# Products of identities in TensorE's planned gaps, and a planner with a changed clock model

## The chip, the cores and the metric

The kernel is one program on one core of a Trainium2 chip. The metric is its device time in microseconds. Four of the core's engines matter here: TensorE (PE, matrix products), VectorE (DVE), ScalarE (ACT) and SyncE (SP, which only issues DMAs). Each runs its own instructions strictly in the order in which the program lists them, and waits on semaphores for the others.

## The reference, cut to what matters

An attention with a local window and a few global rows feeds an MLP with the Mish activation:

```
B, H, Sl, D = 8, 8, 512, 64;  Sg = 32;  window 32
out_g = softmax(q_g k_all^T / 8) v_all                     # 32 global queries see all 544 keys
out_l = softmax([q_l k_g^T | banded q_l k_l^T] / 8) [v_g | v_l]
x     = concat(out_g, out_l) as rows of (B * 544, 512)
h     = x @ w_in            # 512 -> 2048
out   = (h * tanh(softplus(h))) @ w_out      # 2048 -> 512
```

Inputs and output are float32, the two weight matrices float64. Each float32 factor of a large product is cut into two 16-bit parts (high and low), and three 16-bit products are summed in PSUM.

## The kernel before, in words

**Units.** The attention is cut into 128 units: 8 batches x 4 pairs of heads x 4 tiles of 128 local queries. For a unit PE makes the scores (L650 for batches 0 and 1, straight in float32; L657 for the others, in 16-bit parts), DVE adds the mask and takes the row maximum (L663), ACT exponentiates (L672), the probabilities are cut into parts and turned, PE multiplies with V (L741), and after four units DVE normalises (L751). Batch 0 alone is turned on PE: `p_pe` transposes the float32 probabilities with an identity (L696), ACT writes the high part, PE subtracts it from the transposed tile by a product with a negative identity (L701), ACT writes the low part; `x_pe` does the same with the attention's output (L711, L715). Later batches are turned by DMA. The two parts that L741 reads are float16 in every batch.

**The MLP.** There are 17 blocks of 256 rows (two for a batch, one for all global rows), each in 8 steps. `m1_mm` is the first product of a step, 24 matmuls of 256 columns (L873, tile `h`), in two halves of 12; ACT applies Mish (L916), DVE and ACT cut the result into the parts `G` (L329, L327, L929), and `m2_mm` is the second product (L941, tiles `o`), 12 matmuls of 512 columns.

**Weights.** The float64 weights arrive in 32 pieces (k = 0 to 31, 16 for each matrix). DVE makes float32 of each piece with three instructions (L406, L408, L415). `w_stat(k)` then multiplies the piece's upper halves with themselves on PE (L428, four matmuls that add up in the tile `ws`); after 16 pieces `w_norm` takes the diagonal (L435), reduces it over partitions (POOL), computes a power of two (ACT, DVE), and `w_split` cuts the matrix into parts (L460 and L327). No second product can start before `w_norm(1)` is through, and that needs all 32 pieces.

**What sets the order.** Nothing is issued in the order in which it is written. Every piece of work is a task in `Plan` with its engine, an estimated duration, what it reads and writes and a priority. `Plan.order` plays the program through with those estimates and picks, at each step, the task that can start first (priority breaks ties within an engine). The order of starts is the order in which the instructions are emitted, on every engine and on SP's queue, so a changed estimate moves instructions everywhere. For PE the estimate knows a clock: `tensor` cuts time into windows of TICK = 10240/3 ns; a window runs at full speed if at least COLUMNS columns went through PE in the window before, otherwise at half. `rows` is the share at which a task's columns count (0.25 for the float32 scores).

**Rings.** `o` and `h` are two PSUM banks each. `ws` takes an `o` bank for the first 16 pieces, and another for the last 16.

Of the kernel before, what the change touches and what calls it, by code (L numbers as in the profile page):

```python
# [51 lines left out]
class Plan:  # L52
# [6 lines left out]
    DMA_IN, DMA_OUT, DMA_DEPTH = 1500, 400, 5500  # L59
    TICK, COLUMNS = 10240 / 3, 3060  # L60
    LOYAL = 800
    SPARE = 900
    TABLE = 1283

    def __init__(self):
        self.tasks = []
        self.rings = {}
        self.count = {}
        self.last = {}
        self.place = {}  # L70
        self.owner = {}
        self.state = {}
        self.tile = {}
        self.late = 0
        self.slot = None
        self.table = "exp"

    def ring(self, tag, bufs, make):
# [61 lines left out]
    def order(self):  # L140
# [10 lines left out]
        columns = {}  # L151
        served = 0

        def tensor(t, ns, rows):

            while ns > 1e-6:
                k = int(t / self.TICK + 1e-9)
                slow = 1 if columns.get(k - 1, 0) >= self.COLUMNS else 2
                d = min(ns * slow, (k + 1) * self.TICK - t)
                columns[k] = columns.get(k, 0) + d / slow * 2.4 * rows  # L160
                ns -= d / slow
                t += d
            return t
# [26 lines left out]
        for _ in range(N):  # L190
            t, pri, e, n, ns = min(c for c in map(first, free) if c)
            start[n], on[n] = t, e
            if e == ACT:
                self.table = self.tasks[n][7] or self.table
            for x, _ in self.tasks[n][0]:
                queue[x] = [c for c in queue[x] if c[1] != n]
            if e == PE:
                ns = tensor(t, ns, self.tasks[n][6]) - t
            if e == DMA:
                issue, ns = ns[:2]  # L200
                free[e] = t + issue + max(0, served - t - self.DMA_DEPTH)
                served = max(served, t + self.DMA_IN) + ns
                done[n] = served + self.DMA_OUT + (self.SPARE if t > 180000 else 0)
            else:
                free[e] = done[n] = t + ns
            for u in users[n]:
                left[u] -= 1
                if not left[u]:
                    enter(u)
# [3 lines left out]
    def emit(self):  # L213
        for n in self.order():
            engs, fn, deps, after, new, pri, rows, table = self.tasks[n]
            for tag, name in new:
                self.tile[name] = self.rings[tag][1]("_".join(str(x) for x in name))
            if len(engs) > 1:
                fn(self.on[n])
            else:  # L220
                fn()
# [3 lines left out]
def attn_mish_kernel(ctx: ExitStack, tc: tile.TileContext, qt, kt, qt0, kt0, mxs, vm, vg, qg, w1, w2, consts_in, out, w64):  # L225
# [19 lines left out]
    pl = Plan()  # L245
# [172 lines left out]
    WB = 340, 625, 605  # L418

    def w_stat(k):  # L420

        w = k // 16

        def go():
            u = wf(k).bitcast(BF16).rearrange("p (c two) -> p c two", two=2)
            for c in range(4):
                a = u[:, c * 128:(c + 1) * 128, 1]
                T.matmul(X["ws", w][:, :128], a, a, start=(k % 16 == 0 and c == 0), stop=(k % 16 == 15 and c == 3))  # L428
        pl.add(PE, mm(4, 131), go, r=[wkey(*HV[k])], w=[("ws", w)] if k % 16 else (),
               new=() if k % 16 else [("o", ("ws", w))])  # L430

    def w_norm(w):

        m, p = ("wm", w), ("wp", w)
        pl.add(DVE, 210, lambda: V.tensor_tensor_reduce(out=X["wd", w][:, 0, :128],  # L435
                                                        in0=X["ws", w][:, :128], in1=ident, scale=1.0,
                                                        scalar=0.0, op0=ALU.mult, op1=ALU.add, accum_out=X[m]),
               r=[("ws", w), "consts"], new=[("wm", m), ("ob", ("wd", w))])
        pl.add(POOL, 600, lambda: G.partition_all_reduce(X[p], X[m], 128, RED.add), r=[m], new=[("p2", p)])
# [248 lines left out]
    def p_pe(b, hp, t):  # L688
# [3 lines left out]
        def turned():  # L692
            for n in range(4):
                h, c = divmod(n, 2)
                a = c * CHK[t][0]
                T.matmul(X[T_][:, n * 128:n * 128 + 128], X[P][:, h, a:a + 128], ident, start=(n == 0), stop=(n == 3), is_transpose=True)  # L696
        pl.add(PE, mm(4, 262), turned, r=[P, "consts"], new=[("h", T_)])
        cast = lambda part: pl.add(from_ps(512), 0, lambda e: scaled(e, flat(part), X[T_], PSC), r=[T_],
# [5 lines left out]
    def x_pe(b, hp, t):  # L704
# [4 lines left out]
        def turned():  # L709
            for t in ts:  # L710
                T.matmul(X[T_][:, t * 128:(t + 1) * 128], X[x][:, t].rearrange("p h d -> p (h d)"), ident, start=(t == 0), stop=(t == 3), is_transpose=True)  # L711
        pl.add(PE, mm(4, 262), turned, r=[x, "consts"], new=[("h", T_)])
        keys = lambda n: [[n, (hp, half)] for half in range(2)]
# [58 lines left out]
    def g_scores(b, hp, part):  # L772
# [10 lines left out]
        if plain_s(b, hp):  # L783
            kn, kp = pair(b, hp, "kn")
            pl.add(PE, mm(1, 1024) + 150 + (1 - part) * 90, lambda: products((0, 64, [(X["qgraw", b][:, 0, hp, :], X[kn][:, kp])])),
                   r=[[kn, kp], ("qgraw", b)], new=bank(g))
            return
# [372 lines left out]
    for x in ORDER.split():  # L1160
# [7 lines left out]
        elif a == "m":  # L1168
            pl.add(DMA, dma(176), lambda: load(consts, consts_in), w=["consts"])
        elif a == "g":  # L1170
# [83 lines left out]
```

## Time and profile before

| | |
|---|---|
| median of three runs | 959.79 us |
| the profiled execution, device time | 957.52 us |
| its span, first to last instruction | 955.7 us |
| PE busy | 908.4 us (95%) |
| DVE / ACT busy | 668.0 us (70%) / 630.5 us (66%) |
| mean granted PE clock, as the page has it | 0.985 |

The span has two parts. In the first some 137 us batch 0 and 1 of the attention, the conversion of the weights and the first products of the MLP share the chip; after that MLP and attention interleave, and PE is nearly always busy. Busy time of PE counts a slow matmul as fully as a fast one, so it has to be read beside the clock. The clock that the page shows is a list of changes; before the first change in the list it has nothing to go by and shows full speed.

### The profile page before, as it was taken

The numbers are of one execution on the slowest core, as the hardware profiler recorded it, in microseconds if no ns is written. First come the engines' busy times: TensorE is split into PE (matmuls) and PEld (weight loads), VectorE is DVE, ScalarE is ACT, GpSimd is POOL, SyncE is SP. The second block draws the span as 40 slices with busy tenths as digits, with TensorE's granted clock in tenths as the row PEclk, the third lists the DMA queues.
The fourth block names the chain that finished last, engine by engine and source line by source line (L and its number), as shares of the span: only waits on it lengthen the run. The fifth ranks groups of instructions, "written<-read, shape, count | busy, mean of one in ns | idle before, by whom it ended". The sixth has DMA issues, their size and how long they took to land.

```text
span 955.7 us, 20644 instructions
## 1 busy us (share of the span) xinstructions
PE 908.4 (95%) x7988; PEld 628.1 (66%) x7988; DVE 668.0 (70%) x1774; ACT 630.5 (66%) x1283; POOL 19.6 (2%) x28
## 2 busy tenths in 40 slices
PE   7786989999999999999999999999999999999995
PEld 4454666566667767777667766767767776666663
DVE  6789989778998898777877777777776653222221
ACT  4467768776889788767887878887877781212110
POOL 2000000000000000000000000000000000000000
PEclk9978899999999999999999999999999999999998
DMA  9886548978899998756865577757765531000000
GB/s 312 256 286 199 145 134 181 195 173 208 234 230 228 235 230 168 173 127 149 167 160 133 146 152 162 143 137 150 161 125 117 92 77 27 23 1 23 1 23 22
DMA packets 214010, 141.00 MB, mean 148 GB/s; under 512 B 176664, under 2 KB 188184, under 8 KB 212888
## 3 DMA queue, kind: packets, MB, share of 16 engines
q1 hardware_dynamic: 213912, 139.69, 61.4%
q8 instruction: 62, 1.02, 0.5%
q14 instruction: 36, 0.29, 0.1%
HBM read 75.15 MB, written 8.91 MB: 88 GB/s over the span
## 4 chain that ended last, share of the span: by engine, by line
PE 67%; DVE 18%; DMA 8%; ACT 3%; issue 2%; SPq 1%; POOL 0%; DVEq 0%; ACTq 0%
PE o L941 29%; PE h L873 27%; PE U L741 3%; DMA pt<-ph 3%; PE s L657 3%; DMA kn_m<-in_mxs 2%; PE g L781 2%; DVE W L415 2%; DVE W L408 2%; DVE P L663 2%; DMA vraw<-in_vm 1%; PE s L650 1%; DVE W L460 1%; DMA gpt<-gph 1%; DVE mx L528 1%
## 5 line engine op out<-in xcount | busy, mean ns | idle before, releaser
L941 PE MATMUL o<-W,G 128*128 128x512 f16 x1632 | 390.7, 379 | 1.7 <-DVE W L460 0.9
L873 PE MATMUL h<-xh,W 128*128 128x256 f16 x2048 | 375.8, 273 | 2.0 <-ACT e L916 2.0
L873 PEld LDWEIGHTS <-W 128*128 128x128 f16 x3264 | 310.8, 98 | 67.6 <-issue 8.2
L873 PE MATMUL h<-xl,W 128*128 128x256 f16 x1024 | 279.6, 273 | 0.0
L941 PEld LDWEIGHTS <-G 128*128 128x128 f16 x1632 | 156.3, 98 | 146.7 <-issue 4.7
L916 ACT ACTIVATE e<-h,c 128x512 f32<-128x512 f32 (+1 forms) x137 | 91.2, 682 | 121.2 <-PE h L873 115.8
L329 DVE TENSOR_SCALAR G<-e,c 128x512 f16<-128x512 f32 (+1 forms) x122 | 58.7, 481 | 146.2 <-ACT e L916 145.9
L672 ACT ACTIVATE P<-P,nm 128x192 f32<-128x192 f32 (+1 forms) x256 | 118.0, 462 | 52.6 <-DVE nm L663 50.9
L929 DVE SCALAR_TENSOR_TENSOR G<-e,c,G 128x512 f16<-128x512 f32 (+1 forms) x137 | 102.0, 744 | 2.6
L724 DVE SCALAR_TENSOR_TENSOR ph<-P,ph 128x384 f16<-128x384 f32 (+1 forms) x112 | 65.3, 585 | 53.2 <-ACT ph L327 52.7
L663 DVE CUSTOM_DVE_ANT_0 P<-s,consts 128x192 f32<-128x192 f32 (+1 forms) x256 | 91.3, 364 | 13.1 <-PE s L657 8.5
L916 ACT ACT_TABLE_LOAD x61 | 78.3, 1283 | 1.1
L672 ACT ACT_TABLE_LOAD x58 | 74.4, 1283 | 1.0
L741 PEld LDWEIGHTS <-pt 96*128 96x128 f16 (+1 forms) x1536 | 62.2, 99 | 14.8 <-DMA pt<-ph 6.8
L327 ACT ACTIVATE ph<-P 128x384 f16<-128x384 f32 (+1 forms) x112 | 61.0, 546 | 14.5 <-DMA pt<-ph 12.3
L741 PE MATMUL U<-va,pt 128*128 128x64 f16 (+1 forms) x768 | 57.2, 195 | 5.0 <-DMA pt<-ph 3.7
L741 PE MATMUL U<-vc,pt 96*128 96x64 f16 x768 | 56.5, 195 | 0.0
L657 PEld LDWEIGHTS <-qs 128*128 128x128 f16 x384 | 35.7, 98 | 23.4 <-issue 0.8
L672 ACT ACTIVATION_READ_ACCUMULATOR P<-P,nm 128x1 f32 x256 | 47.9, 187 | 0.0
L803 ACT ACTIVATE gP<-g,gmx 64x288 f32<-64x288 f32 x64 | 30.3, 474 | 21.7 <-DVE gmx L798 21.6
L657 PE MATMUL s<-ks,qs 128*128 128x192 f16 (+1 forms) x192 | 42.8, 253 | 0.1
L657 PE MATMUL s<-kl,qs 128*128 128x192 f16 (+1 forms) x192 | 42.8, 253 | 0.0
(121 smaller groups left out, 918.7 us busy)
## 6 DMA issues: line engine op xcount, KB each, us to landing
kraw<-in_kt SPq DMA_DIRECT2D x24, 640.0 KB, 4.7
kn_m<-in_mxs SPq DMA_DIRECT2D x24, 544.0 KB, 5.5
qraw<-in_qt SPq DMA_DIRECT2D x24, 512.0 KB, 4.4
out<-ob SPq DMA_DIRECT2D x34, 256.0 KB, 2.5
vraw<-in_vm SPq DMA_DIRECT2D x8, 1024.0 KB, 6.0
wraw<-in_w SPq DMA_DIRECT2D x16, 512.0 KB, 6.8
W<-in_w SPq DMA_DIRECT2D x16, 512.0 KB, 6.2
vc<-vf SPq DMA_DIRECT2D x32, 128.0 KB, 2.8
```

The lines of the kernel that those rows point to most:

```text
L327: A.activation(out=dst, in_=src, func=AF.Copy, scale=c)
L329: V.tensor_scalar(dst, src, c, None, ALU.mult)
L657: T.matmul(X[s][:, :w], X[qs][:, h, t * 128:(t + 1) * 128], X[k][:, h, c0:c0 + w], start=(i == 0), stop=(i == 1))
L663: pl.add(DVE, 69 + 1.04 * w, lambda: V.tensor_tensor_reduce(out=X[P][:, h, :w], in0=X[s][:, :w], in1=mask[:, m0:m0 + w], scale=-SCALE, sca ...
L672: pl.add(ACT, 94 + 0.832 * w + 186, lambda: A.activation(out=X[P][:, h, :w], in_=X[P][:, h, :w], func=AF.Exp, bias=X[nm], scale=-1.0, accu ...
L724: pl.add(DVE, dve(n), lambda: V.scalar_tensor_tensor(p_part(X[ph], t, 1), p_src(X[P], t), PSC, p_part(X[ph], t, 0), ALU.mult, ALU.subtract ...
L741: T.matmul(X[u][:, t, h, :], X[pt][:k, p * 4 + h * 2 + c, :], X[vx][:k, t, vl, h * 64:(h + 1) * 64], start=(n == 0), stop=(n == 5))
L803: pl.add(ACT, 464, lambda part=part, c0=c0, c1=c1: A.activation(out=X[P][:, c0:c1], in_=X["g", b, hp, part][:64, 0:c1 - c0], func=AF.Exp, ...
L873: T.matmul(X[h][:, f * TB:(f + 1) * TB], wh(i, wl)[:, off:off + 128], X[x][:, d, o:o + TB], start=(n == 0), stop=(n == 11))
L916: chain(blk, i, ACT, 587, lambda a, z: A.activation(out=X[e][:, a:z], in_=hv(blk, i)[:, a:z], func=AF.Mish, bias=0.0, scale=X[c][:, 0:1]), ...
L929: chain(blk, i, DVE, 663, lambda a, z: V.scalar_tensor_tensor(gp(1, blk, i)[:, a:z], X[e][:, a:z], X["c", blk][:, 2:3], gp(0, blk, i)[:, a ...
L941: T.matmul(X[o], gp(g, blk, i)[:, f, t * 128:(t + 1) * 128], wh(8 + i, wl)[:, f * 512:(f + 1) * 512], start=(i == 0 and n == 0), stop=(i = ...
```

## The change

The words that came with the change are: batch 0's P V in fp16 parts; 16-bit products of identities, read by nobody, in TensorE's planned gaps; clock model and constants of the planner set anew. What the diff does:

- The first of these is not in the diff: `p_pe` and L741 compute the same with the same types before and after, save for the `rows` of one task.
- The planner gets a filler: one matmul of 256 bfloat16 columns, both operands the float32 identity read as bfloat16, written to columns 256 to 511 of the `ws` bank. Nobody reads it. It needs only `consts`.
- Before each PE task the planner adds fillers as long as one more would end SLACK = 200 ns before the task's planned start, and one more for each debt: a task with `rows` below 1 adds its duration x (1 - rows) x BOOST to the debt. Fillers stop for good at the first other tile of the ring `o`, which is the first second product of the MLP.
- Both weight statistics and the fillers now share one `o` bank, taken when `consts` is loaded; only the first matmul on it has the start flag.
- COLUMNS goes from 3060 to 3200; `rows` is given to the transposes (0.55) and to the float32 global scores (0.6), which counted fully before. PHASE is 0.

```diff
-    TICK, COLUMNS = 10240 / 3, 3060
+    TICK, COLUMNS, PHASE = 10240 / 3, 3200, 0
     LOYAL = 800
+    SLACK = 200
+    BOOST = 0.2
...
+                if count:
+                    columns[k] = columns.get(k, 0) + d / slow * 2.4 * rows
...
             t, pri, e, n, ns = min(c for c in map(first, free) if c)
+            if any(tag == "o" for tag, _ in self.tasks[n][4]) and n != self.filler[0]:
+                spare = False
+            if e == PE and spare and done[self.filler[0]]:
+                z = free[PE]
+                while debt > 0 or tensor(z, self.filler[1], 1, False) + self.SLACK <= t:
+                    z = tensor(z, self.filler[1], 1)
+                    debt = max(0, debt - self.filler[1])
+                    self.fill[n] = self.fill.get(n, 0) + 1
+                t = max(t, z)
+                debt += ns * max(0, 1 - self.tasks[n][6]) * self.BOOST
...
+            for _ in range(self.fill.get(n, 0)):
+                self.filler[2]()
...
-                T.matmul(X["ws", w][:, :128], a, a, start=(k % 16 == 0 and c == 0), stop=(k % 16 == 15 and c == 3))
-        pl.add(PE, mm(4, 131), go, r=[wkey(*HV[k])], w=[("ws", w)] if k % 16 else (),
-               new=() if k % 16 else [("o", ("ws", w))])
+                T.matmul(X["ws"][:, w * 128:w * 128 + 128], a, a, start=fresh(), stop=(k % 16 == 15 and c == 3),
+                         skip_group_check=True)
+        pl.add(PE, mm(4, 131), go, r=[wkey(*HV[k])], w=[["ws", w]])
...
-        pl.add(PE, mm(4, 262), turned, r=[P, "consts"], new=[("h", T_)])
+        pl.add(PE, mm(4, 262), turned, r=[P, "consts"], new=[("h", T_)], rows=0.55)
...
-                   r=[[kn, kp], ("qgraw", b)], new=bank(g))
+                   r=[[kn, kp], ("qgraw", b)], new=bank(g), rows=0.6)
...
-            pl.add(DMA, dma(176), lambda: load(consts, consts_in), w=["consts"])
+            pl.filler = (len(pl.tasks), mm(1, 262), lambda: T.matmul(
+                X["ws"][:, 256:], ident.bitcast(BF16)[:, :128], ident.bitcast(BF16), start=fresh(), stop=True, skip_group_check=True))
+            pl.add(DMA, dma(176), lambda: load(consts, consts_in), w=["consts"], new=[("o", "ws")])
```

In the changed kernel's order PE gets 347 fillers, each with its weight load. The names in the rows are line, operation, tile written, tiles read and shape; a line of the changed kernel is 16 to 24 higher than the same line before, and L1191 is the filler.

PE at the start of the program, before:

```order
L650 MATMUL s_0_0_0_109<-kn_0_93,qn_0_95 128x192
L650 MATMUL s_0_0_1_113<-kn_0_93,qn_0_95 128x192
L650 MATMUL s_0_1_0_120<-kn_0_93,qn_0_95 128x224
L650 MATMUL s_0_1_1_125<-kn_0_93,qn_0_95 128x224
L696 MATMUL T_0_0_132<-consts,P_74 128x128 x4
```

and now (the first two rows stand 16 times, and then once after each of the others):

```order
L1191 LDWEIGHTS consts
L1191 MATMUL w_s<-consts 128x256
...
L672 MATMUL s_0_0_0_110<-kn_0_93,qn_0_95 128x192
...
L672 MATMUL s_0_0_1_128<-kn_0_93,qn_0_95 128x192
...
L672 MATMUL s_0_1_0_135<-kn_0_93,qn_0_95 128x224
...
L672 MATMUL s_0_1_1_143<-kn_0_93,qn_0_95 128x224
```

The first score now stands behind 16 fillers, which wait for `consts`, the third load of the program.

PE at the first second product, before:

```order
L873 LDWEIGHTS W
L873 MATMUL h_1_1610<-xl_493,W 128x256
L873 LDWEIGHTS W
L873 MATMUL h_1_1610<-xh_467,W 128x256
L941 LDWEIGHTS G_1336
L941 MATMUL o_0_1670<-W,G_1336 128x512
```

and now:

```order
L895 LDWEIGHTS W
L895 MATMUL h_5_2069<-xh_645,W 128x256
L1191 LDWEIGHTS consts
L1191 MATMUL w_s<-consts 128x256
...
L895 LDWEIGHTS W
L895 MATMUL h_6_2144<-xh_645,W 128x256
...
L963 LDWEIGHTS G_1668
L963 MATMUL o_0_2172<-W,G_1668 128x512
```

Before, the first second product follows steps 0 and 1 of the MLP's second block (`h_0`, `h_1`); now it follows steps 0 to 5 and half of step 6. Apart from the 347 fillers and these 108 more L873 matmuls, exactly the same matmuls stand ahead of the first second product in both kernels, in another order. The last 4821 matmuls of PE stand in the same order in both, kind by kind.

SP's queue, where the V parts of the first pair of heads are moved, before:

```order
L316 DMA W<-in_w 128x2x512 x3
L316 DMA va_0_223<-vf_0_199 64x768
L316 DMA vc_84<-vf_0_199 32x768
L316 DMA va_0_223<-vf_0_199 32x768
L316 DMA va_0_223<-vgf_195 32x3x256
L316 DMA va_0_223<-vgf_195 32x256
L316 DMA W<-in_w 128x2x512
```

and now:

```order
L505 DMA_TRANSPOSE gpt_0_364<-gph_88 128x10x64
L332 DMA va_0_293<-vf_0_256 64x768
L332 DMA vc_84<-vf_0_256 32x768
L332 DMA va_0_293<-vf_0_256 32x768
L332 DMA va_0_293<-vgf_248 32x3x256
L332 DMA W<-in_w 128x2x512
L332 DMA va_0_293<-vgf_248 32x256
```

The transpose of the global probabilities, which DVE writes, has moved ahead of the moves of `va_0`; before, it stood after all moves of `va_1`.

More of the change, by code (lines that the diff above doesn't have):

```diff
@@ L76, in __init__ @@
         self.table = "exp"
+        self.fill, self.filler = {}, None
     def ring(self, tag, bufs, make):
@@ L151, in order, with tensor @@
         columns = {}
-        served = 0
-        def tensor(t, ns, rows):
+        served, spare, debt = 0, True, 0
+        def tensor(t, ns, rows, count=True):
             while ns > 1e-6:
-                k = int(t / self.TICK + 1e-9)
+                k = int((t + self.PHASE) / self.TICK + 1e-9)
                 slow = 1 if columns.get(k - 1, 0) >= self.COLUMNS else 2
-                d = min(ns * slow, (k + 1) * self.TICK - t)
-                columns[k] = columns.get(k, 0) + d / slow * 2.4 * rows
+                d = min(ns * slow, (k + 1) * self.TICK - self.PHASE - t)
+                if count:
+                    columns[k] = columns.get(k, 0) + d / slow * 2.4 * rows
                 ns -= d / slow
@@ L418, in attn_mish_kernel, with fresh @@
     WB = 340, 625, 605
+    seen = []
+    def fresh():
+        seen.append(1)
+        return len(seen) == 1
     def w_stat(k):
@@ L435, in w_norm @@
         pl.add(DVE, 210, lambda: V.tensor_tensor_reduce(out=X["wd", w][:, 0, :128],
-                                                        in0=X["ws", w][:, :128], in1=ident, scale=1.0,
+                                                        in0=X["ws"][:, w * 128:w * 128 + 128], in1=ident, scale=1.0,
                                                         scalar=0.0, op0=ALU.mult, op1=ALU.add, accum_out=X[m]),
-               r=[("ws", w), "consts"], new=[("wm", m), ("ob", ("wd", w))])
+               r=[["ws", w], "consts"], new=[("wm", m), ("ob", ("wd", w))])
         pl.add(POOL, 600, lambda: G.partition_all_reduce(X[p], X[m], 128, RED.add), r=[m], new=[("p2", p)])
@@ L711, in turned @@
                 T.matmul(X[T_][:, t * 128:(t + 1) * 128], X[x][:, t].rearrange("p h d -> p (h d)"), ident, start=(t == 0), stop=(t == 3), is_transpose=True)
-        pl.add(PE, mm(4, 262), turned, r=[x, "consts"], new=[("h", T_)])
+        pl.add(PE, mm(4, 262), turned, r=[x, "consts"], new=[("h", T_)], rows=0.55)
         keys = lambda n: [[n, (hp, half)] for half in range(2)]
```

## The prediction, on record before the changed kernel ran

> **What bounds the kernel now.** I read the windows view first, cut where the granted clock changes, then the groups of instructions on PE at two clocks, then the waits. Columns of the windows: length, busy us (instructions) of PE, PE's weight loads, DVE, ACT and POOL, granted clock, DMA share, GB/s.
>
> ```profile
> 0.00:39.20 39.20, 25.80 (x153) 16.63 (x154) 26.60 (x80) 15.07 (x41) 6.79 (x13) 1.00 0.87 282
> 39.20:59.70 20.50, 15.96 (x164) 10.33 (x160) 19.51 (x55) 13.44 (x37) 0.00 (x0) 0.99 0.97 286
> 59.70:69.90 10.20, 10.09 (x52) 6.65 (x52) 8.22 (x31) 6.28 (x20) 0.76 (x1) 0.51 0.78 284
> 69.90:76.80 6.90, 4.79 (x50) 3.32 (x48) 6.24 (x18) 5.91 (x15) 0.00 (x0) 0.98 0.48 151
> 76.80:83.60 6.80, 5.35 (x55) 3.74 (x55) 6.80 (x12) 4.48 (x8) 0.00 (x0) 0.52 0.91 320
> 83.60:97.20 13.60, 8.23 (x65) 4.90 (x65) 13.60 (x43) 10.70 (x29) 0.00 (x0) 0.99 0.55 168
> 97.20:104.10 6.90, 6.75 (x44) 4.30 (x44) 6.90 (x19) 4.68 (x12) 0.00 (x0) 0.52 0.85 228
> 104.10:136.70 32.60, 30.13 (x268) 25.09 (x268) 28.70 (x74) 20.54 (x39) 1.31 (x2) 1.00 0.44 124
> 136.70:200.00 63.30, 60.87 (x521) 36.51 (x521) 54.65 (x144) 50.85 (x109) 1.63 (x2) 1.00 0.79 174
> 200.00:386.00 186.00, 181.69 (x1746) 127.92 (x1745) 162.86 (x424) 150.74 (x302) 5.71 (x6) 1.00 0.94 216
> 386.00:920.00 534.00, 532.93 (x4723) 372.80 (x4721) 327.27 (x874) 344.14 (x673) 3.36 (x4) 1.00 0.50 109
> 920.00:955.70 35.70, 25.78 (x166) 15.95 (x164) 6.68 (x12) 3.69 (x6) 0.00 (x0) 0.92 0.05 15
> ```
>
> From 136.70 on PE is the bound: it idles 2.4 us to 200, 4.3 to 386 and 1.1 to 920. Before, the bound is shared: DVE is busy all of 76.8 to 83.6 and 83.6 to 104.1, PE all of 59.7 to 69.9. That last stretch has the clock at 0.51, though PE is busy 10.09 of 10.20 us: busy time alone does not hold the clock.
>
> The first row's 1.00 can't be right. The same instructions before 39 us (first two rows) and in 39.4 to 59.5 us (last two):
>
> ```profile
> L696 PE MATMUL T<-consts,P 128*128 128x128 f32 x20 | 5.5, 431 | 0.0
> L701 PE MATMUL T<-pt,pid 128*128 128x512 f16 x4 | 2.4, 597 | 0.2
> L696 PE MATMUL T<-consts,P 128*128 128x128 f32 x20 | 3.1, 276 | 0.0
> L701 PE MATMUL T<-pt,pid 128*128 128x512 f16 x6 | 2.3, 380 | 0.5 <-ACT pt L327 0.5
> ```
>
> A 512-column product takes 597 against 380 ns, a difference of 217, about half of what 512 columns last at half speed. So PE ran at half clock up to 39.2 us, and again in the three stretches at 0.51 and 0.52. The waits of PE and of DVE in the first 137 us:
>
> ```profile
> PE ws L428 <- DVE W L415: 13.1, 14, 3.5
> PE Tx L711 <- DVE x L751: 3.2, 3, 1.8
> DVE pid L1174 <- DMA consts<-in_consts: 4.3, 1, 4.3
> DVE x L751 <- PE U L741: 4.1, 1, 4.1
> DVE P L663 <- PE s L650: 3.4, 5, 1.1
> DVE vmx L498 <- DMA vraw<-in_vm: 2.0, 1, 2.0
> ```
>
> PE waits mostly for DVE's conversion of weights; DVE waits 7.5 us for PE.
>
> **The change, part by part.** The last 4821 matmuls stand in the same order in both kernels, from about 386 us on, where PE idles 1.1 us in 534. So what decides is how much sooner that common tail begins. I follow it in two steps: when the first second product starts (now 136.70), and what is done by then.
>
> *Done by then.* The order shows the same matmuls ahead of it, plus 108 more L873, which later need not be done, plus 347 fillers. What 256 columns take is the distance of starts:
>
> ```profile
> 102.75 0.63 PE L873 MATMUL h<-xh,W 128*128 128x256 f16 x2
> 103.39 0.59 PE L873 MATMUL h<-xh,W 128*128 128x256 f16 x2
> 106.18 0.28 PE L873 MATMUL h<-xh,W 128*128 128x256 f16 x1
> 107.72 0.38 PE L873 MATMUL h<-xh,W 128*128 128x256 f16 x2
> L873 PE MATMUL h<-xh,W 128*128 128x256 f16 x2048 | 375.8, 273 | 2.0 <-ACT e L916 2.0
> ```
>
> Between the first two lie three starts (0.64 us, 213 ns each, half clock), between the third and the fourth fourteen (1.54 us, 110 ns, full); the last row, the page's group, has 273 ns as the mean record of one. The 108 are worth 11.8 us of lead, the 347 fillers cost 37.8 us.
>
> *PE's way there.* Up to 136.70 PE is busy 107.1 us (sum of the column). 48.0 of them at half clock (25.80 + 10.09 + 5.35 + 6.75) would be 24.0 at full: 83.1. With the 11.8 and 37.8 it is 132.7. The fillers need `consts`, and the first scores now stand behind 16 of them:
>
> ```profile
> 4.57 2.73 PE L650 MATMUL s<-kn,qn 64*128 64x192 f32 x8 [4.57 <-DMA qn<-in_qt]
> 5.19 0.62 DVE L1174 TENSOR_SCALAR pid<-consts 128x128 f16<-128x128 f32 x1 [4.33 <-DMA consts<-in_consts]
> 33.38 0.36 PE L741 MATMUL U<-va,pt 96*128 96x64 f16 x3
> ```
>
> So PE starts at 5.2, and 16 fillers at 213 ns end at 8.6. When does the clock rise? Before, it rose at 39.2, some 5.9 us after PE had gone over to dense 16-bit work at 33.3 (last row). The same here gives 11.1, so 5.9 us are run at half speed, a loss of 2.95. The sum is 5.2 + 132.7 + 3.0 = 140.9 if PE never waits. The busy sum is an upper end, since a lone matmul's record lasts 0.16 us beyond its spacing (273 against 110); where work is dense such tails vanish, so 136 to 141.
>
> The Trainium skill (TensorE: Matmul & The Clock Gate, Part 1, what's actually happening) has the clock released after one busy window of about 3.4 us, free-running against the kernel. By that the loss would be 1.7 to 3.4 us instead of 2.95, and the sum 139.6 to 141.3. The trace's steps at 59.7, 69.9, 76.8, 83.6, 97.2 and 104.1 are multiples of 3.4 us apart, as it says; none falls on a multiple of 3.4 counted from the program's start, as PHASE = 0 assumes.
>
> *DVE's way there.* It is busy 116.6 us up to 136.70 and idle 20.1. By its order, 20 instructions more now stand ahead of the first split of the second matrix:
>
> ```profile
> L929 DVE SCALAR_TENSOR_TENSOR G<-e,c,G 128x512 f16<-128x512 f32 x8 | 6.0, 745 | 0.1
> L329 DVE TENSOR_SCALAR G<-e,c 128x512 f16<-128x512 f32 x6 | 2.9, 484 | 0.0
> L528 DVE TENSOR_REDUCE mx<-kn_m 128x1 f32<-128x1088 f32 x3 | 3.8, 1282 | 1.6 <-DMA kn_m<-in_mxs 1.5
> ```
>
> Four each of the first two (3.0 and 1.9), one of the third (1.3), the rest small, together about 1: 7.2 us, so 123.8. Idle: the first score starts at 8.6 instead of 4.57, so the first row maximum comes 4.0 us later, which covers the 2.0 us wait for `vraw`: 20.1 + 4.0 - 2.0 = 22.1, in all 145.9. From that goes what a full clock saves of DVE's 7.5 us of waits for PE: all of it gives 138.4, nothing 145.9. I take half, 142: the wait of 4.1 stands at U of the first heads, where 25 fillers (2.7 us) and, on SP, the transpose that waits for DVE's `gph` ahead of `va_0` now stand in front, so most of it stays; the 3.4 for scores came mainly while PE was slow. DVE, not PE, is then the later of the two, and the start moves from 136.7 to 142, 5.3 later, with 11.8 more done: a lead of 6.5 us. Bounds are 138.4 (lead 10.1) and 145.9 (2.6).
>
> *After it.* PE's idle time of 2.4 + 4.3 up to 386 may grow, since PE comes sooner and DVE must follow. DVE has 217.5 us of work there in 249.3, 87%; with 7.2 done before and 6.5 us less time it has 210.3 in 242.8, 87% again. So most of the lead should last. But the order of batch 1 has changed, and each of its waits, for turned probabilities among them, can fall differently: from nothing to 4, I take 2.
>
> *Costs that I put at nothing.* The fillers' weight loads run beside products (PEld is less busy than PE in every row). The shared `ws` bank makes two fillers wait for DVE's reading of it, once each, at a time when DVE has just been waited for; if not covered, under 1 us. ACT has the same work. Batch 0's P V is what it was.
>
> Sum: -6.5 + 2 = -4.5 us. The profiled execution lasted 957.52 (span 955.7, 1.8 around it), so 953.0 for its like; it lay 2.3 below the median, and against 959.79 the forecast is **955.3 us**.
>
> **The rivals.**
>
> *PE never waits.* Every gap was a planned one and DVE follows at once: start at 138.4, lead 10.1, nothing given back, 949.7. For it: DVE's waits for PE vanish with a fast clock. Against: two engines, PE then some 96% busy on its way (132.7 of 138.4) and DVE some 89% (123.8 of 138.4), each waiting for the other, have never run without waits here; PE waits 13.1 us for conversions in the trace.
>
> *DVE takes it all.* DVE's way is 145.9, and the other 2.6 us of lead go into batch 1: 959.8, no change. For it: DVE was fully busy in 76.8 to 104.1 while PE idled, so a faster PE there buys nothing.
>
> *Fillers in the way* (slower). A filler can't be skipped: where the planned gap has already passed, because PE is late, it delays the next product by 110 ns. The place is the whole stretch from 8.6 to the first second product; PE starts some 4 us late against a plan that begins at time 0 and has 0.2 us of slack at a gap. If the 13.7 us that PE idles in 39.2 to 104.1 (lengths less busy times of the six rows) are still waited for in spite of the fillers, PE's way is 140.9 + 13.7 = 154.6, and 154.6 - 136.7 - 11.8 = 6.1 later: 965.9. It decides once the start is past 148.5. For it: the DVE work that PE waits for is longer than before. Against: DVE's way is some 9 us shorter than that.
>
> *The clock does not rise.* If products of a nearly empty identity don't count, 347 at 213 ns are 74 us, and the other 95 us of PE's work take up to twice as long: the start is past 200, over 1010 us. Against: the trace's clock rose on the small 64-column products of U; that it heeds values, nothing shows.
>
> **How the numbers follow.** The forecast has 0.46, PE never waits 0.17, DVE takes it all 0.20, fillers in the way 0.14, no rise 0.03. About 0.2%, 1.9 us, is what a measurement can tell here. Faster is the first two, 0.63; same 0.20; slower 0.17. The range runs from the best case, 949, to half of the slower one, 962.5 (start at 151); past the ends lie the rest of that rival, the clock's and a little of the best: 0.2.
>
> **What would show it.** The first L696 and L701 after some 12 us take 276 and 380 ns, and no clock of 0.5 comes before the tail. PE's busy time is near 97% from 8.6 us on, with DVE's waits for PE at 4 us or less. The first second product (now L963) starts at 142, not past 148.5; 386 us of the old trace come at 381 to 382, and from there everything is shifted evenly. Wrong would be PE idle over 8 us before the first second product beside its 37.8 us of fillers, or a lead there that is gone by the common tail.

## The result: slower by 0.7%

| | before | changed |
|---|---|---|
| median, us | 959.03 (958.44 to 959.84) | 964.48 (962.97 to 969.29) |
| ratio | | 1.0071, 95% interval 1.0048 to 1.0094 |
| span of the profiled execution, us | 955.7 | 962.7 |
| first second product of the MLP, us | 136.7 | 153.75 |

The forecast was 955.3 us with a range of 949.0 to 962.5. The time lies above the range, on the side to which 0.17 had been given. The ratio takes in all runs, and the medians alone would give 1.0057: of the seven runs of the changed kernel four lie at 962.97 to 964.48 us with a mean granted clock of 0.995 or 0.996, and three at 968.10 to 969.29 us with 0.990 or 0.991. In a second series, beside some of the experiments, the same kernel stood at 1.0103 (1.0063 to 1.0142) of the kernel before.

### The profile page after: what moved, and what is told of

Same layout as the page of the kernel before. It is cut to its first block, busy times and chain, and to the rows that moved or that the text cites. A ratio compares the mean times of both kernels' runs of the same rounds, so it can differ in the third digit from the quotient of the medians.

```text
span 962.7 us, 21334 instructions
## 1 busy us (share of the span) xinstructions
PE 935.3 (97%) x8335; PEld 652.7 (68%) x8335; DVE 672.9 (70%) x1776; ACT 623.9 (65%) x1277; POOL 15.2 (2%) x28
## 4 chain that ended last, share of the span: by engine, by line
PE 80%; DMA 8%; DVE 7%; ACT 3%; issue 1%; SPq 0%; ACTq 0%; DVEq 0%
PE h L895 32%; PE o L963 31%; DMA pt<-ph 5%; PE U L763 4%; PE s L679 3%; PE w_s L1191 3%; PE s L672 2%; PE g L803 2%; PE gu L852 1%; DVE W L424 1%; DVE W L431 1%; DMA vraw<-in_vm 1%; DMA gpt<-gph 1%; ACT L938 1%; PE T L718 1%
## 5 line engine op out<-in xcount | busy, mean ns | idle before, releaser
L895 PE MATMUL h<-xh,W 128*128 128x256 f16 x2048 | 373.9, 273 | 1.7 <-ACT e L938 1.5
L895 PEld LDWEIGHTS <-W 128*128 128x128 f16 x3264 | 311.5, 98 | 64.6 <-issue 6.2
L895 PE MATMUL h<-xl,W 128*128 128x256 f16 x1024 | 278.9, 272 | 0.0
L345 DVE TENSOR_SCALAR G<-e,c 128x512 f16<-128x512 f32 (+1 forms) x122 | 58.6, 480 | 145.3 <-ACT e L938 144.8
L685 DVE CUSTOM_DVE_ANT_0 P<-s,consts 128x192 f32<-128x192 f32 (+1 forms) x256 | 91.5, 365 | 23.6 <-PE s L672 12.5
L1191 PE MATMUL w_s<-consts 128*128 128x256 bf16 x347 | 56.1, 281 | 5.7 <-DMA consts<-in_consts 5.7
L1191 PEld LDWEIGHTS <-consts 128*128 128x128 bf16 x347 | 33.3, 99 | 23.3 <-issue 13.4
```

Of the source, the lines that this page charges most:

```text
L345: V.tensor_scalar(dst, src, c, None, ALU.mult)
L685: pl.add(DVE, 69 + 1.04 * w, lambda: V.tensor_tensor_reduce(out=X[P][:, h, :w], in0=X[s][:, :w], in1=mask[:, m0:m0 + w], scale=-SCALE, sca ...
L895: T.matmul(X[h][:, f * TB:(f + 1) * TB], wh(i, wl)[:, off:off + 128], X[x][:, d, o:o + TB], start=(n == 0), stop=(n == 11))
L1191: pl.filler = (len(pl.tasks), mm(1, 262), lambda: T.matmul(X["ws"][:, 256:], ident.bitcast(BF16)[:, :128], ident.bitcast(BF16), start=fres ...
```

## The profile after

The first lines of the page, and its group of fillers (busy time and mean of one; idle time ahead):

```profile
span 962.7 us, 21334 instructions
PE 935.3 (97%) x8335; PEld 652.7 (68%) x8335; DVE 672.9 (70%) x1776; ACT 623.9 (65%) x1277; POOL 15.2 (2%) x28
L1191 PE MATMUL w_s<-consts 128*128 128x256 bf16 x347 | 56.1, 281 | 5.7 <-DMA consts<-in_consts 5.7
```

PE is busier than before, 935.3 against 908.4 us, in spite of a faster clock. The windows view, cut at the changes of the clock, at the first second product (153.7) and where the common tail begins (392.6):

```profile
0.00:10.10 10.10, 4.40 (x18) 2.69 (x18) 1.28 (x2) 1.28 (x1) 6.29 (x12) 1.00 0.84 304
10.10:80.00 69.90, 69.14 (x636) 49.25 (x635) 59.32 (x174) 39.57 (x111) 0.73 (x2) 1.00 0.79 254
80.00:120.00 40.00, 39.48 (x345) 28.47 (x345) 37.80 (x102) 29.38 (x69) 0.00 (x0) 1.00 0.56 158
120.00:153.70 33.70, 31.79 (x299) 28.06 (x297) 30.22 (x70) 18.39 (x25) 1.68 (x3) 1.00 0.42 126
153.70:225.10 71.40, 66.27 (x548) 36.16 (x546) 56.92 (x143) 49.21 (x110) 0.35 (x1) 1.00 0.86 187
225.10:228.50 3.40, 3.40 (x40) 2.27 (x37) 2.69 (x12) 3.08 (x12) 0.00 (x0) 0.50 0.88 208
228.50:392.60 164.10, 162.70 (x1584) 117.11 (x1584) 151.86 (x397) 132.63 (x277) 2.83 (x6) 1.00 0.94 224
392.60:927.00 534.40, 532.85 (x4723) 373.18 (x4721) 326.63 (x872) 346.63 (x672) 3.37 (x4) 1.00 0.50 109
```

The clock rises at 10.1 us and falls again only at 225.1, for one stretch of 3.4 us: the fillers did what they can do for the clock. From 10.1 to 153.7 PE is busy 140.41 of 143.60 us. It hardly waits any more, it has too much to do, and VectorE, with 127.34 of these 143.60 us, waits for it. The row of the waits up to 153.75 (in all, times, longest), and the same of before, where the prediction quotes 3.4:

```profile
DVE P L685 <- PE s L672: 11.7, 15, 3.5
```

What PE does up to the first second product, by groups, is the surprise. First before (up to 136.7), then after:

```profile
L650 PE MATMUL s<-kn,qn 64*128 64x192 f32 (+1 forms) x88 | 25.7, 509 | 7.5 <-DMA qn<-in_qt 4.6 <-ACT gP L803 1.7 <-DVE nm L663 1.3
L428 PE MATMUL ws<-W 128*128 128x128 bf16 x128 | 16.0, 261 | 13.6 <-DVE W L415 13.1 <-DVE gs L813 0.4
L696 PE MATMUL T<-consts,P 128*128 128x128 f32 x64 | 13.5, 349 | 0.0
```

```profile
L672 PE MATMUL s<-kn,qn 64*128 64x192 f32 (+1 forms) x88 | 27.5, 393 | 0.0
L450 PE MATMUL w_s<-W 128*128 128x128 bf16 x128 | 12.4, 220 | 1.5 <-DVE W L431 1.2
L718 PE MATMUL T<-consts,P 128*128 128x128 f32 x64 | 9.8, 276 | 0.0
```

Weight statistics and turns got shorter with the faster clock. The float32 scores did not: one record takes 393 instead of 509 ns, and yet the 88 of them (two to a score, 44 scores) take 27.5 instead of 25.7 us. The timeline tells why. First the scores of two heads in the kernel before, then scores of the same shape in the changed kernel:

```profile
48.83 0.65 PE L650 MATMUL s<-kn,qn 64*128 64x224 f32 x4
49.41 0.39 PE L701 MATMUL T<-pt,pid 128*128 128x512 f16 x1
```

```profile
41.09 0.64 PE L672 MATMUL s<-kn,qn 64*128 64x224 f32 x2
41.66 0.28 PE L1191 MATMUL w_s<-consts 128*128 128x256 bf16 x1
41.78 0.38 PE L723 MATMUL T<-pt,pid 128*128 128x512 f16 x1
42.09 0.64 PE L672 MATMUL s<-kn,qn 64*128 64x224 f32 x2
```

Four records, two scores, in 0.65 us before; two records, one score, in 0.64 us after. A score reads 64 rows, and the two heads lie on different halves of the 128 partitions: standing next to each other, both run at once. In the kernel before that happens ten times on the way to the first second product (in the trace the records of such a pair start 70 ns apart or less), in the changed kernel not once, since a filler that uses all 128 rows, or other work, stands between. The Trainium skill (TensorE: Matmul & The Clock Gate, Part 3, packing small matmuls) has products whose operands start at different partitions run concurrently, their starts about 4 ns apart. Most of the pairs here start 6 or 7 ns apart, so the trace agrees in kind.

Next to a float32 score a filler itself also takes longer. The timeline of the changed kernel at its first scores:

```profile
10.15 0.28 PE L1191 MATMUL w_s<-consts 128*128 128x256 bf16 x1
10.36 0.59 PE L672 MATMUL s<-kn,qn 64*128 64x192 f32 x2
10.88 0.28 PE L1191 MATMUL w_s<-consts 128*128 128x256 bf16 x1
11.10 0.64 PE L672 MATMUL s<-kn,qn 64*128 64x224 f32 x2
```

From the filler's start to the score's are 0.21 us, not 0.11. By distances of starts in the trace the 347 fillers take 45.4 us: 234 in front of another filler at full clock 25.6 (109 ns each), 15 at half clock 3.2, 37 in front of a float32 score or global score 7.7 (about 0.21 each), the other 61 8.9.

## The experiments

Theory 1: the loss is TensorE's work, lengthened above all by pairs of scores that no longer run side by side. Theory 2: it is the fillers' own time. Theory 3: VectorE's way sets the start of the second products anyway. Theory 4: it is the new order, that is the planner's constants. All experiments start from the changed kernel. "Start" is the first second product, "work" and "idle" are TensorE's up to it (from its first product on), "tail" is its last product, all from each run's profiled execution.

| kernel | fillers | clock rises | work | idle | start | tail | median | ratio to before (95%) |
|---|---|---|---|---|---|---|---|---|
| before | 0 | 39.0 | 107.1 | 25.0 | 136.7 | 945.8 | | |
| changed | 347 | 10.1 | 144.9 | 3.2 | 153.75 | 952.3 | 964.48 | 1.0071 (1.0048 to 1.0094) |
| again | 347 | 11.6 | 145.0 | 2.8 | 154.6 | 951.8 | 965.14 | 1.0103 (1.0063 to 1.0142) |
| pairs | 347 | 16.1 | 139.8 | 5.4 | 152.1 | 948.9 | 960.25 | 1.0009 (0.9993 to 1.0025) |
| pairs_late | 347 | 12.7 | 139.7 | 5.7 | 149.8 | 946.7 | 960.19 | 1.0025 (1.0013 to 1.0036) |
| none | 0 | 46.1 | 125.5 | 24.4 | 154.4 | 953.4 | 963.79 | 1.0049 (1.0029 to 1.0069) |
| nostart | 331 | 23.6 | 148.5 | 4.4 | 157.25 | 954.2 | 964.10 | 1.0063 (1.0039 to 1.0088) |
| gaps | 273 | 21.2 | 136.2 | 7.5 | 149.0 | 947.8 | 957.42 | 0.9989 (0.9967 to 1.0012) |
| gaps_ns | 257 | 16.5 | 132.8 | 7.5 | 144.9 | 944.0 | 955.24 | 0.9972 (0.9955 to 0.9989) |
| gaps_half | 128 | 22.2 | 121.4 | 18.8 | 144.8 | 941.2 | 953.56 | 0.9953 (0.9939 to 0.9968) |
| half_split | 141 | 23.2 | 127.9 | 13.5 | 146.0 | 944.3 | 956.83 | 0.9981 (0.9967 to 0.9996) |
| gaps_quarter | 64 | 35.9 | 126.7 | 19.8 | 151.05 | 946.8 | 958.19 | 0.9990 (0.9972 to 1.0008) |
| planonly | 0 | 12.3 | 96.0 | 28.0 | 128.6 | 945.8 | 957.64 | 0.9991 (0.9978 to 1.0005) |
| boost0_ns | 221 | 23.7 | 119.2 | 11.3 | 135.0 | 955.1 | 965.74 | 1.0069 (1.0045 to 1.0093) |

All but the kernel before, planonly and boost0_ns have the same 348 L895 matmuls ahead of the start; for them the break-even with before is the prediction's 148.5. In none, gaps_quarter, planonly and boost0_ns the clock falls again before the start (planonly at 19.1, boost0_ns at 30.5). Start, work, idle and tail are those of one execution each: two executions of the same kernel, changed and again, differ by 0.9 us at the start; `consts` landed 1.1 us later in the second.

### Pairs of scores kept together (pairs)

```diff
+            score = rows == 0.25 and engs[0][0] == PE
+            owed += self.fill.get(n, 0)
+            if engs[0][0] == PE and not (score and scored):
+                for _ in range(owed):
+                    self.filler[2]()
+                owed = 0
+            if engs[0][0] == PE:
+                scored = score
```

> The changed kernel with the same order and the same 347 fillers, but a filler that stands between two float32 scores (L672 behind L672) is issued behind the second one. Before, two such scores of the two heads of a pair, on 64 rows each, start 6 ns apart and run side by side (575 ns for both); in the changed kernel none does up to 153 us. Theory 1 (the fillers keep pairs of scores from running side by side): 13 of the 44 scores ahead of the first second product stand next to another one, 13 x 0.575 = 7.5 us of TensorE's time come back, the first second product starts at 146 to 147 instead of 153.8, and the time is 957 to 958. Theory 2 (the loss is the fillers' own time, 45 us against 37.8): the same fillers run, so the start stays within 1 us of 153.8 and the time within 1.5 of 964.5. Theory 3 (VectorE's way sets the start): TensorE gets the 7.5 us and then waits for VectorE; the start comes at 150 or later, the time is 961 or more.

The groups up to the start, the fillers and the scores:

```profile
L1198 PE MATMUL w_s<-consts 128*128 128x256 bf16 x347 | 53.1, 283 | 6.8 <-DMA consts<-in_consts 6.8
L679 PE MATMUL s<-kn,qn 64*128 64x192 f32 (+1 forms) x88 | 20.9, 414 | 1.0 <-DVE nm L692 0.7 <-ACT gP L832 0.2
```

The same fillers and the same 88 records of scores, which now take 20.9 instead of 27.5 us; TensorE's work falls by 5.1 us, of 7.5 expected, with the clock up 6 us later than in the changed kernel. The ratio falls from 1.0071 and 1.0103 to 1.0009, so by the times most of the loss is this, and theory 2 falls as the whole cause. The way to the time is seen only in part. In the profile 1.65 us reach the start, 152.1 where 146 to 147 was expected: `consts` landed 1.15 us later in this execution, and PE idles 2.2 us more. At the tail pairs is 3.4 us ahead. Some 0.9 of that is there at 275 us, where the same matmul is compared; the other 2.5 come from single waits further on, which only the changed kernel has in these two executions, most of them for turned probabilities. The longest, in the changed kernel:

```profile
583.82 0.26 PE L763 MATMUL U<-va,pt 96*128 96x64 f16 x3 [0.89 <-DMA pt<-ph]
```

The expected 957 to 958 is missed by 2.3, and the 961 or more of theory 3 is not reached, though its start (150 or later) is.

### No filler at all (none), and no filler in the plan (planonly)

none leaves out the two lines that issue the fillers. planonly:

```diff
-        served, spare, debt = 0, True, 0
+        served, spare, debt = 0, False, 0
```

> The changed kernel's order without any filler: the 347 products are left out, everything else is issued in the same order. The rest of TensorE's work ahead of the first second product is 99.4 us at full clock, 92 with the pairs of scores side by side again. If the fillers do their work on the clock, it drops to half in several stretches before 154 us as in the kernel before, and the first second product comes at 148 to 152 (before: 136.7, with 11.8 us less to do ahead of it: 148.5), the time is 959 to 963. Theory 1 and 2 (too much TensorE work with fillers): at or under 961. If the fillers' clock is worth more than they cost, it is slower than 964.5.

> The changed kernel with a planner that knows no filler: COLUMNS 3200, the lower shares for transposes and global scores and the shared bank stay; no filler is planned or issued, so the order is a new one. If the constants alone do harm (theory 4: the loss is in the new order, not in the fillers), it takes 962 or more. If they are harmless, it is within 3 of the kernel before, 957 to 962, with half-clock stretches like those before.

Without fillers the same order loses its clock; two rows of the windows of the run none:

```profile
46.10:70.00 23.90, 18.88 (x209) 12.63 (x208) 22.35 (x66) 17.35 (x47) 0.38 (x1) 1.00 0.85 282
70.00:97.30 27.30, 23.63 (x145) 15.51 (x143) 23.81 (x71) 17.38 (x44) 0.00 (x0) 0.50 0.64 214
```

For 27.3 us PE runs at half speed (busy for 23.63 of them), and the start comes at 154.4, later than expected and as late as with all fillers. The time, 963.79, is just above the 959 to 963 expected and above the 961 that theories 1 and 2 allow. So in this order the 347 fillers just about pay for themselves: what they give by the clock they take back as work. planonly ends within 0.1% of the kernel before: the constants alone do no harm. Its order is another one than the changed kernel's; that this order does no harm by itself either is shown by gaps_half below, which has it and is faster than the kernel before. With both, theory 4 falls.

### Only the fillers of planned gaps (gaps), and without those of the start (gaps_ns, nostart)

gaps counts the fillers that a debt called for and leaves them out; gaps_ns also leaves out the first 16; nostart leaves out only these.

```diff
+                    self.owe[n] = self.owe.get(n, 0) + (debt > 0)
...
+            if first and self.fill.get(n, 0):
+                first, self.fill[n] = False, 0
-            for _ in range(self.fill.get(n, 0)):
+            for _ in range(self.fill.get(n, 0) - self.owe.get(n, 0)):
```

> The changed kernel's order with fewer fillers: those that the planner adds for a debt (one behind nearly every float32 product or turn) are left out, those of planned gaps stay, 273 instead of 347. Theory 1: pairs of scores run side by side again (7.5 us), and 74 fillers at 0.11 to 0.21 us are gone (8 to 15 us): TensorE's way ends by 140, so that VectorE sets the start at 142 to 147, time 954 to 958, if the clock holds. Theory 2: 8 to 15 us less, the start at 140 to 146. Theory 3: the start stays at 150 or later. If the debt fillers are what holds the clock, it drops to half within 10 to 150 us and the gain is partly lost.

> As the run without debt fillers (273 left, first second product at 149.0 in its profile, VectorE busy 40.0 of 40 us from 80 to 120), and without the 16 fillers at the start either (257 left). Theory 3 (VectorE's way now sets the start, and it begins late, since the first score stands behind 16 fillers and `consts`): the first score starts at 4.6 instead of some 9, VectorE's first row maximum comes 4 us sooner, the first second product at 145 to 146, the time 953 to 955. If the clock counts instead: with nothing dense ahead of 25 us it rises late, TensorE's first 30 us run at half speed, VectorE waits for it there, the start stays at 148 to 150 and the time at 957 to 959.

> The changed kernel without the 16 fillers at the very start; all else in the same order. If TensorE's work is the bound (pairs broken up), 16 x 0.213 = 3.4 us fall away and TensorE starts about 1 us sooner, so the first second product comes at 149 to 150 and the time is 960 to 961. If those 16 are what raises the clock early, the clock rises some 6 to 11 us later than the 10 us seen, which costs half of that, 3 to 5 us: no gain, 963 to 965.

One row of the windows of gaps, and one of gaps_ns:

```profile
80.00:120.00 40.00, 37.78 (x356) 28.49 (x354) 40.00 (x106) 30.60 (x70) 0.00 (x0) 1.00 0.57 168
```

```profile
80.00:120.00 40.00, 38.22 (x354) 29.48 (x355) 39.93 (x107) 29.51 (x68) 0.00 (x0) 1.00 0.50 150
```

With 74 fillers fewer VectorE is busy all the time from 80 to 120: the bound is passing to it, as theory 3 has it and gaps_half below shows. gaps starts at 149.0, between the expectations (142 to 147, and 150 or later), since its VectorE begins late; its time, 957.42, is within the 954 to 958 of theory 1. The first row maximum in the timeline of VectorE, gaps first, then gaps_ns:

```profile
10.00 0.36 DVE L686 CUSTOM_DVE_ANT_0 P<-s,consts 128x192 f32<-128x192 f32 x1 [4.21 <-PE s L673]
```

```profile
5.68 0.36 DVE L689 CUSTOM_DVE_ANT_0 P<-s,consts 128x192 f32<-128x192 f32 x1
```

4.3 us sooner at the beginning, 4.1 us sooner at the start (149.0 to 144.9, where 145 to 146 was expected): from the first row maximum to the start both take the same time, 139.0 and 139.2 us, so the 16 fillers ahead of the first score, with the wait for `consts`, cost VectorE's way their whole length. The time, 955.24, is in the range expected, but the intervals of the two ratios overlap, so that the times alone do not tell gaps_ns from gaps. In nostart the same edit gains nothing that can be told (1.0063 against 1.0071 and 1.0103): there TensorE's work is the bound, the pairs are still broken up, and the clock rises at 23.6 instead of 10.1, as the second of its expectations had it; the first, 149 to 150, is refuted by 157.25.

### The fillers of the start behind the first scores (pairs_late), and the changed kernel once more (again)

pairs_late is pairs with the fillers of the start held back until five scores are issued.

> As the run in which no filler stands between two float32 scores (347 fillers, start at 152.1 in its profile: 6.9 until `consts` landed, 139.8 of work, 5.4 idle), but with the fillers of the start behind the first five scores. TensorE begins at 4.5 and VectorE's first row maximum comes some 4 us sooner. If TensorE's work is still the bound: 4.5 + 139.8 + 3 to 5 idle gives 147 to 149, time 955 to 957. If what the scores need first (ring of three banks, VectorE) was the wait anyway: 150 to 152, 958 to 960.

> The changed kernel itself once more, beside the three next kernels on one chip. With the first series (ratio 1.0071 to the kernel before, pairs of scores broken up) and the run in which only those pairs were mended (1.0009), theory 1 expects 1.005 to 1.009 here too; if the difference between those two was one of chips, 0.999 to 1.003. The profile again shows no two scores side by side, and about 45 us of fillers.

In its profiled execution pairs_late starts at 149.8 and ends TensorE's work 2.2 us sooner than pairs, but the medians are the same (960.25 and 960.19), and the ratios' intervals overlap: whether it helps stays open. The 147 to 149 and 955 to 957 expected of a bound TensorE are missed; the time, 960.19, stands at the upper end of the other expectation, 958 to 960. With 139.7 us of work and 5.7 idle TensorE is still busy nearly all the time; gaps_ns, with 90 fillers less, starts at 144.9. The run again confirms the loss.

### Half and a quarter of the fillers, and pairs broken up on purpose (gaps_half, gaps_quarter, half_split)

```diff
+            count = self.fill.get(n, 0) - self.owe.get(n, 0)
-            for _ in range(self.fill.get(n, 0)):
+            for _ in range((total + count) // 2 - total // 2):
                 self.filler[2]()
+            total += count
```

on top of gaps_ns; gaps_quarter has 4 for 2. half_split is gaps_half with one filler more between two scores that stand next to each other where the plan had a filler, from the first other filler on.

> As the run with neither debt fillers nor starting ones (257 fillers, 31.8 us, first second product at 144.9, time 955.24, VectorE busy 39.93 of 40 us from 80 to 120), with every second of its fillers left out: 128 remain, 16 us less of TensorE's time. If VectorE now sets the start and the clock holds, nothing is gained from the 16 us: the start at 143 to 145, 953.5 to 955.5. If TensorE's work is still the bound: 135 to 140, 947 to 950. If 128 are too few for the clock, it falls to half in the gaps: the start at 147 or later, 957 or more.

> As the run with 128 fillers (every second one of the planned gaps from the first unit of the second pair of heads on; start of the first second product 144.8, 953.56 us), with every fourth instead: 64 fillers, 7 us less of TensorE's time. If VectorE's way sets the start and the clock needs no more than this: 143.5 to 145, 952 to 954. If the clock falls to half between the sparse fillers, as without any (154.4, 963.79), TensorE is late for VectorE: 147 to 152, 956 to 961.

> The run with 128 fillers, and 13 more, each put between two float32 scores that stood next to each other there. By theory 1, some 8 pairs that ran side by side no longer do (0.575 us each) and 13 fillers cost 0.21 us each: 4.6 + 2.7 = 7.3 us more of TensorE's time, 121.4 becomes 128 to 129. If TensorE's 18.8 us of idle time cover that and only VectorE's way counts: the start within 1.2 us of 144.8, 953 to 955. If VectorE waits for the later score each time (0.5 to 0.7 us, 13 times): 148 to 152, 957 to 961.

gaps_half has 11.4 us less work for TensorE than gaps_ns, and the same start (144.8 and 144.9): VectorE's way sets it, theory 3's hit. Of these runs it has the lowest time, 953.56 us, 0.47% under the kernel before; its interval overlaps with that of gaps_ns. The 2.8 us that it ends ahead of gaps_ns in the profiles arise behind the start, mostly where PE waits less for turned probabilities; the waits of 145 to 235, gaps_ns and then gaps_half:

```profile
PE U L767 <- DMA pt<-ph: 3.6, 3, 2.3
```

```profile
PE U L769 <- DMA pt<-ph: 1.5, 3, 0.7
```

With a quarter the clock goes, as the second expectation has it: it falls at 80.3, 94.0 and 148.6, the row of 80 to 120 has it at 0.79, and VectorE is no longer always busy there:

```profile
80.00:120.00 40.00, 36.22 (x278) 25.48 (x276) 35.61 (x97) 28.37 (x66) 0.00 (x0) 0.79 0.50 136
```

half_split is the pairs' effect by itself; the scores' group up to the start, of gaps_half and of half_split:

```profile
L678 PE MATMUL s<-kn,qn 64*128 64x192 f32 (+1 forms) x88 | 23.8, 437 | 5.7 <-DMA qn<-in_qt 4.6 <-DVE nm L691 1.0
```

```profile
L682 PE MATMUL s<-kn,qn 64*128 64x192 f32 (+1 forms) x88 | 29.4, 440 | 5.8 <-DMA qn<-in_qt 4.6 <-DVE nm L695 1.2
```

13 fillers more, and the scores take 5.6 us longer; TensorE's work grows by 6.5 us (7.3 expected). Where it has 18.8 us of idle time to spare the start moves by 1.2 us only, as expected. The time, 956.83, is 3.3 us more than that of gaps_half and lies between the two expectations; the profiled executions differ by 1.2 us at the start and 3.1 at the tail, so some 1.9 us arise behind the start. They are not lost in batch 1: at 266 us the same matmul is 1.0 us later, as at the start, and the rest comes mostly from single waits for turned probabilities that only half_split has there. The two longest, in half_split:

```profile
499.85 0.26 PE L862 MATMUL gu<-gpt,va 128*128 128x64 f16 x3 [0.78 <-DMA gpt<-gph]
675.24 0.26 PE L773 MATMUL U<-va,pt 96*128 96x64 f16 x3 [0.59 <-DMA pt<-ph]
```

Both kernels issue the same matmuls there in the same order; whether the broken pairs or chance put these waits there, the runs do not tell.

### Planned for what is issued (boost0_ns)

```diff
-    BOOST = 0.2
+    BOOST = 0
...
-                while debt > 0 or tensor(z, self.filler[1], 1, False) + self.SLACK <= t:
+                while warm and tensor(z, self.filler[1], 1, False) + self.SLACK <= t:
                     z = tensor(z, self.filler[1], 1)
...
+                warm = True
```

> A planner with BOOST 0 and no fillers ahead of the first TensorE task, so the order is planned for what is issued: 221 fillers, and 252 L895 matmuls ahead of the first second product instead of 348 (10.5 us less; break-even with the kernel before at a start of 138.0 instead of 148.5). If the order of the changed kernel was spoilt by planning for fillers that lengthen TensorE's work, this one starts the first second product at 131 to 135 and takes 953 to 956. If VectorE's way is the bound in any order: 136 to 138, 957 to 959.

The start is where it was expected, 135.0, 3.0 ahead of its break-even of 138.0, and the time is 10 us worse than expected. The lead is lost in batch 1. One row of the windows of before, one of boost0_ns, and the first of the latter's waits in that stretch:

```profile
200.00:300.00 100.00, 95.81 (x923) 66.83 (x922) 88.27 (x237) 79.86 (x165) 3.16 (x3) 1.00 0.90 215
```

```profile
200.00:300.00 100.00, 86.44 (x810) 59.06 (x809) 85.14 (x217) 66.45 (x141) 2.59 (x4) 0.93 0.97 224
PE U L764 <- DMA pt<-ph: 9.2, 5, 3.8
```

PE is idle 13.6 us there instead of 4.2, 9.2 of them for probabilities that the DMA turns, and the clock falls twice on the way. A lead at the start is worth something only if the order behind it can follow.

## Why the prediction was wrong, step by step

**PE's way, 140.9.** This step failed. The forecast was 5.2 + 94.9 (83.1 + 11.8) + 40.8 (37.8 + 3.0) with PE never waiting; measured are 5.7 + 99.5 + 45.4 + 3.2 of idle time = 153.8. The 4.6 us more of the second term are the scores: "48.0 of them at half clock would be 24.0 at full" took PE's busy time for a sum of instructions. It is the time in which at least one runs, and in it ten pairs of scores count once. The prediction went on to call this sum "an upper end" and let it fall to 136; with pairs in it, it was too low. Where the pairs stay (pairs), the scores take 5.2 us less by distances of starts, which leaves 94.3. The 4.6 of the third term are mostly the fillers' places: beside a float32 score a filler takes 0.21, not 0.11 us. The sentence "Costs that I put at nothing" looked at the fillers' weight loads and banks, but not at what they stand between; the order, in which a filler follows each of the first scores, was quoted in the text ahead of it.

**The clock.** Right in the profiled execution: it rose at 10.1 (forecast 11.1) and stayed up to the start. That products of an identity count is shown by the run none, which has the same order without them and loses the clock at 70.0; the rival by which they do not count is refuted. That the 16 at the start are what raised it is not shown: in gaps_ns it rose at 16.5, before the first filler. Not foreseen was the one stretch at half speed at 225.1, behind the last filler, which costs some 1.7 us (half of its 3.4, an estimate).

**DVE's way, 142, bounds 138.4 and 145.9.** Too short as well, which PE's way hides in the changed kernel. gaps_ns and gaps_half, where TensorE's work is short enough, start at 144.9 and 144.8, but without the late first score, for which the forecast had 4.0 us less the 2.0 that it takes from the wait for `vraw`. With it the start is at 149.0, in gaps, 7 us later than forecast and past the upper bound. One row of its windows, up to the start:

```profile
0.00:149.04 149.04, 136.21 (x1219) 102.39 (x1220) 126.32 (x346) 87.87 (x204) 8.78 (x17) 1.00 0.70 211
```

VectorE is busy 126.3 us (123.8 in the forecast) and so idle 22.7 (18.2 in it, and 22.1 where a full clock saves nothing): nothing of the saving is left to see, and there was 2.5 us more to do. The clock of gaps rises at 21.2 us, not 11.1; what an earlier rise would have saved VectorE, no run separates. As this run stands, its start lies at the 148.5 at which nothing is gained, and gaps gains nothing that can be told (0.9989): by this run, mending PE's way alone would not have made the forecast of 955.3 true. The term of 4.0 us for the late first score is confirmed by gaps and gaps_ns (4.3 at the row maximum, 4.1 at the start); the 2.0 taken off for `vraw` are not. The forecast had counted the late score as a cost without asking for the version without it.

**Behind the start.** Right in kind: 17.1 us later with 11.8 us more done are 5.3, and at the beginning of the common tail it is 6.1 (386.6 to 392.7 for the same matmul), 0.8 of change where 2 were taken. From there to 643 us it wanders between 5.3 and 6.9 with single waits, and from 643 us on the distance is 6.5 throughout, so the tail is shifted nearly evenly, as forecast.

**The rivals.** The slower one named the point from which it decides, 148.5, and a price of 965.9 with a start at 154.6. Measured are 964.48 and 153.75. That its figures come so near is luck, since its mechanism is not what happened: PE does not wait on in spite of the fillers (3.2 us of idle time, not 13.7), its own work is longer, by the 9.2 us above. Its chance of 0.14 was too low: with a PE some 96% busy by the sum itself, each error in that sum goes straight to the end.

## What to carry to other kernels

Busy time of PE hides products that run side by side, so before something is put between two of them, look in the timeline at how many records fall into one product's time. Filling gaps to hold the clock paid here only while another engine was the bound: 128 of the 347 fillers held the clock, once it had risen, as well as all of them, and the rest made TensorE the bound. A filler ahead of the first work of a chain delays that chain by its whole length: leave it out (putting it behind that work, in pairs_late, showed no gain that can be told).

## What the runs showed of the hardware

Being busy did not suffice to raise the clock. In gaps PE is busy without a pause from its first filler to the rise at 21.2; the window view has

```profile
5.30:21.20 15.90, 15.89 (x53) 9.32 (x53) 6.58 (x26) 6.30 (x20) 1.95 (x3) 1.00 0.82 306
```

and from the timeline of PE there:

```profile
5.31 3.59 PE L1192 MATMUL w_s<-consts 128*128 128x256 bf16 x16 [5.31 <-DMA consts<-in_consts]
...
15.01 1.00 PE L673 MATMUL s<-kn,qn 64*128 64x192 f32 x2
...
21.34 0.59 PE L673 MATMUL s<-kn,qn 64*128 64x192 f32 x2
```

A 192-column score takes 1.00 us at 15.01 and 0.59 after the rise, so the clock was at half (the 1.00 in the clock's column only says that no change was recorded yet). The first 3.59 us are 16 fillers, the rest float32 products and turns and two 16-bit products. In the changed kernel the same 16 fillers at the start, beginning at 5.7 instead of 5.3 us, were followed by the rise at 10.1. The Trainium skill (TensorE: Matmul & The Clock Gate, Part 1, what's actually happening) has the clock released after one busy window of about 3.4 us. By that the rise in gaps would have come at 12.1 at the latest (an estimate: 5.3 and two such windows); it came at 21.2, so by these rows being busy is not enough.

What it takes these runs do not settle. That float32 products can't raise the clock would be too much to say: in gaps_ns it rose at 16.5, behind the same float32 products and turns and two 16-bit ones, before the first filler was run,

```profile
16.91 0.28 PE L1195 MATMUL w_s<-consts 128*128 128x256 bf16 x1
```

and in planonly, which has no filler, at 12.3. Where the products fall in a window may decide, and the differences between executions of one kernel may come from there; neither was tried.
